# Constant masks by VectorE comparisons in place of GpSimd's affine_select, in a gated attention mix

## The chip, the cores and the metric

The kernel runs on one core of one Trainium2 chip. A core has five engines, each with an instruction stream of its own: TensorE (PE; its weight loads are listed as PEld), VectorE (DVE), ScalarE (ACT), GpSimd (POOL) and SyncE (SP, which here only issues DMAs). They wait for one another by semaphores. The metric is the device time of one execution in microseconds (us), the median of several runs. Beside it stands one execution taken by the hardware profiler, whose records the views of the profile are made of.

## The reference, cut to what matters

The input x has 2048 rows of 512 numbers. Two blocks are computed of it and mixed by a gate for each row.

```
g = sigmoid((x * gate_w).sum(-1))          # one number for each row
a = softmax_attention(x, A_wqkv, A_wo)     # 32 heads of 16, softmax over 2048 keys
b = linear_attention(x, B_wqkv, B_wo)      # phi(t) = (t > 0 ? t + 1 : exp(t)) + 1e-6
out = g * a + (1 - g) * b
```

In block A, for each head, `p = softmax(q k^T / 4)` and `o = p v`; the heads' outputs, side by side, are multiplied by `A_wo`. In block B `kv = phi(k)^T v` and `z = sum(phi(k))` are formed for each head, and `o = phi(q) kv / (phi(q) z)`.

## The kernel before, in words

Block A is most of the work: 32 heads x 2048 queries x 2048 keys of exponentials. Heads are taken in four groups of eight (`t8`), queries in four chunks of 512 (`qc`), keys in 16 blocks of 128. A round handles four of the eight heads of a group (half 0: heads 0, 2, 4, 6; half 1: the others) for one chunk of queries. TensorE makes scores, keys on the partitions and queries along the row, with the four heads in four strips of 32 rows of the array; a strip holds the 16 rows of the wanted head and 16 rows of zeros (tile `Qpad`, four slots). The scores are then turned into exponentials, most of them by ScalarE (L2069, three or two banks of 512 at once, into `PT`), the others by VectorE, which writes an integer whose bits approximate the exponential (L1563, into `DP`), with shifted copies of it made by GpSimd's INT64_ADD (L1607) or by VectorE (L1604). TensorE multiplies `PT` and `DP` with the values (`Vaug`, which carries a column of ones for the sums). Block B's steps, the output projection and the normalisation are woven in between.

The order of instructions on each engine is fixed when the program is built: a planner in the kernel keeps a clock for each engine, adds up estimated durations (`dur`) and picks the next step by them. On the chip each engine works through its list in order. `op(engine, fn, reads, writes, dur)` records one instruction; the waits come from what it reads and writes (L168, L100). TensorE is taken to be in order with itself and waits for no result of its own; VectorE, ScalarE and GpSimd do wait on their own semaphore for an earlier result that they need. One rule more counts here (L530): each GpSimd instruction also waits for the last VectorE instruction recorded before it that reads no PSUM, since the two share a path to SBUF.

The start of the program, which the change touches, runs so:

- ScalarE's queue issues the load of the first 512 rows of x (tile `xn0`, which lies in `PT`), then of half the columns of the other rows (`xnat`, in `phi`). SP's queue issues the three slices of A's weights for the first head group (`wA0`, in `outt`: Q, K, V), six DMA transposes of x into `xT`, then all of A's weights (`wA`) and the gate's weights, later the Q rows for the other `Qpad` slots (L634), and B's weights.
- GpSimd sets `dummy`, `warm` and `identb` (L702, L733, L734), builds the constant masks (L735 to L744), and sets the upper part of `Vaug`, `ones1`, `dev` and `O_sb` (L758 to L762).
- The masks are four tiles. `identb` (128x128) is the identity that TensorE needs to transpose. `maskK` (128x8) has a one where partition p belongs to head column j, that is where 16 j <= p < 16 j + 16. `maskQ` (128x1) is one on the partitions of the even heads. `blockmask` (128x128) is `maskK` with each column repeated 16 times.
- VectorE sets the lower part of `Vaug` (L750 to L752) and three slots of `Qpad` (L754), and sums four columns of `maskK` into `maskQ` (L756).
- TensorE multiplies `warm` nine times (L1877), transposes the first 512 rows of x with `identb` (16 transposes, L692), and VectorE and ScalarE copy them to `xT`, two each (L1907, L1905). Then come the projections of Q and of the first 256 keys, two more multiplications of `warm`, and the first scores. Q goes to `Qpad` slot 0 through `maskQ` (L885) and unmasked to `Qs` (L889); K goes to `KT` (L854, L857), V to `Vaug` (L912, with scaled copies L923).
- The first exponential (L2069) follows the first three scores.

`maskK` and `blockmask` themselves are used much later, in block B (L1025, L1044), and so is `KVbd`, the tile that the change uses as scratch.

Of the kernel before, what the change touches and what calls it, by code (L numbers as in the profile page):

```python
# [9 lines left out]
ALU = mybir.AluOpType  # L10
AX = mybir.AxisListType
# [203 lines left out]
def bass_gated_mix__mha_block__linear_attn_block__prompt_kernel(  # L215
# [16 lines left out]
    NQC = S // 512  # L232
# [16 lines left out]
    with ExitStack() as es:  # L249
# [18 lines left out]
        identb = SB([128, 128], BF16, "identb")  # L268
        maskK = SB([128, 8], FP32, "maskK")
        maskQ = SB([128, 1], FP32, "maskQ")  # L270
        blockmask = SB([128, 128], BF16, "blockmask")
# [11 lines left out]
        Z0 = V20 + 2 * (NG4 - 1) * (V2C + PAD)  # L283
        Vraw = SB([128, Z0 + 32], BF16, "Vaug")
# [30 lines left out]
        KVbd = SB([128, NCC, 128], BF16, "KVbd")  # L315
# [38 lines left out]
        DV = _Eng("dve", SEM("s_dve"))  # L354
        PO = _Eng("pool", SEM("s_pool"))
# [25 lines left out]
        r_gw, r_ident, r_const, r_mask, r_bmask, r_dummy = R("gw"), R("ident"), R("const"), R("mask"), R("bmask"), R("dm")  # L381
        r_maskQ = R("maskQ")
# [3 lines left out]
        r_V = [[R(f"V{p}_{v}") for v in range(NQC)] for p in range(2)]  # L386
# [17 lines left out]
        r_KVbd, r_Zsel = R("KVbd"), R("Zsel")  # L404
# [143 lines left out]
        def op(E, fn, reads=(), writes=(), dur=0.2, issue=None):  # L548
            settle(reads, writes)
            return _emit(E, fn, reads, writes, dur, issue)  # L550
# [140 lines left out]
        def f_tr(o, i):  # L691
# [12 lines left out]
           dur=1.6)  # L704
# [9 lines left out]
        for t in range(1, NQC):  # L714
            for cc in range(NCD):
                dma(xT[:, cc, 512 * t:512 * (t + 1)], x2[512 * t:512 * (t + 1), 128 * cc:128 * (cc + 1)], semXT[cc][t],
                    writes=[r_xT[cc][t]], total_after=16, transpose=True, E=SP, lands=5.5)
# [7 lines left out]
            return [r_xT[c][t] for c in range(NCC)]  # L725


        def select(view, base, pattern, mult, w):

            op(PO, lambda: nc.gpsimd.affine_select(out=view, in_=view, compare_op=ALU.is_ge, fill=0.0, base=base,  # L730
                                                   pattern=pattern, channel_multiplier=mult), reads=[w], writes=[w])

        op(PO, lambda: nc.gpsimd.memset(warm[:], 0.0), writes=[r_warm])  # L733
        op(PO, lambda: nc.gpsimd.memset(identb[:], 0.0), writes=[r_ident])  # L734
        op(PO, lambda: nc.gpsimd.affine_select(out=identb[:], in_=identb[:], compare_op=ALU.not_equal,  # L735
                                               fill=1.0, base=0, pattern=[[-1, 128]], channel_multiplier=1),
           reads=[r_ident], writes=[r_ident])
        op(PO, lambda: nc.gpsimd.memset(maskK[:], 1.0), writes=[r_mask])
        select(maskK[:], 0, [[-16, 8]], 1, r_mask)
        select(maskK[:], 15, [[16, 8]], -1, r_mask)  # L740
        op(PO, lambda: nc.gpsimd.memset(blockmask[:], 1.0), writes=[r_bmask])
        bm = blockmask[:].rearrange("p (j c) -> p j c", c=16)
        select(bm, 0, [[-16, 8], [0, 16]], 1, r_bmask)
        select(bm, 15, [[16, 8], [0, 16]], -1, r_bmask)  # L744
        n0 = NQC * VG

        def ones(g0, g1):
            return Vraw[:, g0 * VG:g1 * VG].rearrange("p (g x) -> p g x", x=VG)[:, :, 0:VG - PAD].rearrange(
                "p g (n c) -> p g n c", c=VC)[:, :, :, 16:17]
        op(DV, lambda: nc.vector.memset(Vraw[:, 0:n0], 0.0), writes=r_V[0], dur=1.2)  # L750
        op(DV, lambda: nc.vector.memset(ones(0, NQC), 1.0), writes=r_V[0], dur=0.2)
        op(DV, lambda: nc.vector.memset(Vraw[:, Z0:Z0 + 32], 0.0), writes=r_V[0], dur=0.1)  # L752
        for i in range(1, NQS):
            op(DV, lambda i=i: nc.vector.memset(Qpad[:, i, :], 0.0), writes=[r_Q[i]], dur=0.49)  # L754

        op(DV, lambda: nc.vector.reduce_sum(maskQ[:, 0:1], maskK[:].rearrange("p (a two) -> p two a", two=2)[:, 0, :], axis=AX.X),  # L756
           reads=[r_mask], writes=[r_maskQ], dur=0.2)
        op(PO, lambda: nc.gpsimd.memset(Vraw[:, n0:Z0], 0.0), writes=r_V[1] + r_V2, dur=4.0)  # L758
        op(PO, lambda: nc.gpsimd.memset(ones(NQC, NG), 1.0), writes=r_V[1], dur=0.4)
        op(PO, lambda: nc.gpsimd.memset(ones1[:], 1.0), writes=[r_ones1], dur=0.1)  # L760
# [880 lines left out]
        for t8 in range(1, NT8):  # L1641
            base = GPR * r_of(t8 - 1, 0)
# [287 lines left out]
        for st, w in ((step_Q(0, 0, early=True), r_wA0[0]), (step_K(0, 0, early=True, on_act=True, n=256), r_wA0[1])):  # L1930
            b = rot_bank()
            pair.append((st, w, b, st.pieces(b)))
        for c in range(2):
            for st, w, b, pcs in pair:
                fns, _, dur, mac, mode = pcs[c]
# [50 lines left out]
        while True:  # L1986
# [20 lines left out]
            while len(us) < SLOTS[g % 2][1]:  # L2007
                if len(us) == 2 and (away or lend is not None):
                    break
                if len(us) == 2 and g > last_stage:  # L2010
                    own, j3 = b0 + 2 in more, peek()
                    load = dve_load(PE.t)
                    if more and load < (RING_LATE if behind_by() > BEHIND else RING_LOAD):
                        js = [j for j in range(4) if j not in [u % 4 for _, u in us]]
                        three = own and len(more) > 1 and load >= TWO_LOAD and j3 in js
                        c = can_claim(PE.t, [j for j in js if not three or j != j3])
# [42 lines left out]
            for c, eb in extras:  # L2059
# [4 lines left out]
                     dur=QK_T, mac=0.053 * len(fns), mode="rows")  # L2064
            for c, eb in extras:
# [5 lines left out]
               reads=[r_bank[b0 + k] for k in range(len(us))], writes=mine + ([r_xn0] if 3 <= g < 5 else []),  # L2071
               dur=d_act(n), issue=0.055 + n * 8.34e-4)
# [59 lines left out]
        while pv_pending:  # L2132
            if not pv_step(PE.t, force=True):
# [9 lines left out]
                 writes=[r_bank[tbank]], dur=0.3)  # L2143
# [3 lines left out]
           reads=[r_bank[tbank], r_OT[NT8 - 1][lastq]], writes=[r_OT[NT8 - 1][lastq]], dur=0.68)  # L2147
# [4 lines left out]
           writes=[r_bad], dur=0.25)  # L2152
# [5 lines left out]
        for k in order:  # L2158
            tb = 4 * lastq + k
            pe_macro([f_mm(bank_ap(free[k]), OT[:, NT8 - 1, 128 * tb:128 * (tb + 1)], woA[:, NT8 - 1, :], start=(k < NPRE))],  # L2160
                     reads=[r_OT[NT8 - 1][lastq], r_woA], writes=[r_bank[free[k]]], dur=MM512)
        for k in range(NPRE, 4):
# [3 lines left out]
               reads=[r_bank[free[k]], r_g], writes=[r_outl[k]], dur=0.6)  # L2166
            dma(out2[128 * tb:128 * (tb + 1), :], outl[:, k, :], semL[k], reads=[r_outl[k]], total_after=16, E=AC)
        for k in range(NPRE):
# [4 lines left out]
               reads=[r_bank[free[k]], r_pre[k], r_g], writes=[r_outl[k]], dur=d_psum(512))  # L2173
            dma(out2[128 * tb:128 * (tb + 1), :], outl[:, k, :], semL[k], reads=[r_outl[k]], total_after=16, E=SP)
            if k == 0:
                op(DV, lambda: nc.vector.scalar_tensor_tensor(out=bad, in0=dev[:, 1, :], scalar=OK_MID - OK_HALF, in1=bad,  # L2176
                                                              op0=ALU.is_lt, op1=ALU.max),
                   reads=[r_dev, r_bad], writes=[r_bad], dur=0.28)
                pe_macro([f_mm(bank_ap(tbank)[0:1, 0:128], ones1[:], bad)], reads=[r_bad, r_ones1],
                         writes=[r_bank[tbank]], dur=0.1)  # L2180
        op(DV, lambda: nc.vector.reduce_max(flag[0:1, 0:1], bank_ap(tbank)[0:1, 0:128], axis=AX.X),  # L2181
           reads=[r_bank[tbank]], writes=[r_flag], dur=0.28)
# [178 lines left out]
```

## Time and profile before

| | before |
|---|---|
| time, median of 3 runs | 678.46 us (678.44 to 678.69) |
| time of the profiled execution | 678.79 us |
| its span, first to last instruction | 677.0 us |
| ScalarE busy | 655.0 us (97%) |
| TensorE busy | 649.5 us (96%) |
| VectorE busy | 565.1 us (83%) |
| GpSimd busy | 343.0 us (51%) |
| mean granted TensorE clock | 0.99 |

The span is shorter than the execution's own time; what lies around it (1.79 us) is start and end of the program. Busy time is that of recorded instructions; a matmul's end is modelled, so a busy TensorE is not TensorE at its peak. In a timeline row stand the start and the length in us, engine, line, operation, output tile <- input tiles, shape and count; in square brackets the idle time ahead of it and what ended that. In a row of the chain stand start, length, and what the chain ran through; "issue" is time in which the engine waited for nothing that the profile shows. In a group's row the part behind the bar is busy time in us and mean ns of one, and then idle time ahead of the group's instructions. L1907 is line 1907 of the kernel; L685 and L692 are the helpers that issue every matmul and every transpose. SPq and ACTq are DMA issues on the queues of SP and ScalarE.

### The profile page before, as it was taken

The page shows a single profiled execution, that of the slowest core. Times are in us where ns is not written, and L with a number is a line of the kernel's source. Part 1 is how long each engine was busy: PE and PEld are TensorE (multiplying, and loading weights), DVE is VectorE, ACT ScalarE, POOL GpSimd, SP SyncE. Part 2 cuts the span into 40 slices and gives each one's busy share as a digit, 9 for nine tenths or more (in the row PEclk, how much of TensorE's full clock was granted, in tenths as well). Part 3 has the DMA queues.
Part 4 walks back from the last instruction along what each step waited for, and adds up shares of the span by engine and source line. Part 5 has one row for each costly group of instructions (what it writes and reads, how often), then busy time and mean ns, then how long its engine had stood idle before and what let it go on. Part 6 is the DMA issues. An engine that isn't in the chain of part 4 may idle for free.

```text
span 677.0 us, 19101 instructions
## 1 busy us (share of the span) xinstructions
PE 649.5 (96%) x8028; PEld 199.0 (29%) x8028; DVE 565.1 (83%) x952; ACT 655.0 (97%) x710; POOL 343.0 (51%) x339
## 2 busy tenths in 40 slices
PE   4999999999999999999999999999999999999997
PEld 2422222333223323333222323233222322222223
DVE  2478889889998987977889999899989987888793
ACT  1999999999999999999999999999999999999996
POOL 2235465453545464544555555555555455656551
PEclk7999999999999999999999999999999999999999
DMA  9800100101000011200001011011102201020111
GB/s 218 229 26 3 32 4 11 25 3 26 10 18 19 9 27 33 53 16 17 19 1 34 18 26 27 10 34 25 35 9 38 53 22 45 12 46 19 28 27 48
DMA packets 44816, 22.96 MB, mean 34 GB/s; under 512 B 33976, under 2 KB 40568, under 8 KB 44728
## 3 DMA queue, kind: packets, MB, share of 16 engines
q1 hardware_dynamic: 42712, 20.12, 13.1%
q10 hardware_dynamic: 2016, 1.57, 0.9%
q8 instruction: 66, 1.08, 0.7%
q14 instruction: 22, 0.18, 0.1%
HBM read 8.00 MB, written 2.10 MB: 15 GB/s over the span
## 4 chain that ended last, share of the span: by engine, by line
ACT 93%; PE 4%; issue 2%; DVE 1%; POOL 0%; POOLq 0%; ACTq 0%
ACT PT L2069 90%; PE ps L685 4%; ACT epool L968 2%; PE ps L692 0%; DVE DP L2171 0%; DVE epool L1402 0%; DVE epool L1403 0%; DVE KT L857 0%; POOL identb L735 0%; DVE DP L2176 0%; DVE flag L2181 0%; POOL identb L734 0%; POOL warm L733 0%; POOL dummy L702 0%; ACT eg L952 0%
## 5 line engine op out<-in xcount | busy, mean ns | idle before, releaser
L2069 ACT ACTIVATE PT<-ps 128x1024 bf16<-128x1024 f32 (+1 forms) x670 | 643.1, 1160 | 1.0 <-PE ps L685 0.9
L1563 DVE TENSOR_SCALAR DP<-ps 128x512 int16<-128x512 f32 x664 | 439.4, 686 | 72.4 <-PE ps L685 66.3
L1607 POOL INT64_ADD DP<-DP x320 | 334.6, 1055 | 307.3 <-DVE DP L1563 223.7
L685 PE MATMUL ps<-Qpad,KT 32*128 32x512 bf16 x2048 | 262.9, 384 | 12.1 <-ACT PT L2069 6.4
L685 PE MATMUL ps<-DP,Vaug 128*32 128x512 f16 x1987 | 203.7, 384 | 1.7 <-DVE oraw L1304 1.5
L685 PE MATMUL ps<-PT,Vaug 128*32 128x512 bf16 x1373 | 169.9, 384 | 0.5 <-DVE Vaug L912 0.5
L685 PEld LDWEIGHTS ps<-Qpad,KT 32*128 32x128 bf16 x2048 | 66.0, 91 | 272.9 <-ACT PT L2069 245.5
L685 PEld LDWEIGHTS ps<-DP,Vaug 128*32 128x32 bf16 x1987 | 49.2, 95 | 61.2 <-issue 37.8
L685 PEld LDWEIGHTS ps<-PT,Vaug 128*32 128x32 bf16 x1373 | 40.6, 95 | 46.9 <-issue 36.0
L685 PE MATMUL ps<-warm 128*32 128x512 bf16 (+2 forms) x221 | 39.9, 391 | 1.1 <-POOL warm L733 1.1
L685 PE MATMUL ps<-xT,wA 128*32 128x512 bf16 x432 | 32.5, 384 | 0.0
L968 ACT ACTIVATE epool<-ps 128x512 bf16<-128x512 f32 x32 | 23.3, 730 | 0.0
L1304 DVE COPY oraw<-ps 128x512 f32<-128x512 f32 x31 | 21.2, 682 | 0.5 <-PE ps L685 0.4
L685 PE MATMUL ps<-wB,xT 128*32 128x512 bf16 x256 | 19.7, 384 | 0.0
L685 PE MATMUL ps<-xT,wB 128*32 128x512 bf16 x256 | 19.7, 384 | 0.0
L685 PE MATMUL ps<-woA,OT 128*32 128x512 bf16 (+1 forms) x226 | 19.1, 384 | 0.0
L973 DVE SCALAR_TENSOR_TENSOR phi<-ps,epool 128x512 bf16<-128x512 f32 x24 | 16.4, 682 | 0.1
L857 DVE CAST KT<-ps 128x512 bf16<-128x512 f32 (+1 forms) x16 | 10.7, 667 | 5.6 <-PE ps L685 5.6
L685 PE MATMUL ps<-wA,xT 128*128 128x128 bf16 x192 | 14.9, 220 | 0.0
L685 PEld LDWEIGHTS ps<-warm 128*32 128x32 bf16 (+1 forms) x221 | 9.9, 98 | 13.7 <-issue 12.1
L912 DVE CAST Vaug<-ps 128x512 bf16<-128x512 f32 x16 | 10.9, 684 | 3.6 <-PE ps L685 3.6
L685 PEld LDWEIGHTS ps<-wA,xT 128*128 128x128 bf16 x192 | 10.8, 98 | 5.4 <-issue 5.0
(104 smaller groups left out, 238.7 us busy)
## 6 DMA issues: line engine op xcount, KB each, us to landing
rbc<-oraw SPq DMA_DIRECT2D x16, 256.0 KB
OT<-in_A_x_dram SPq DMA_DIRECT2D x4, 512.0 KB, 6.5
Qpad<-Qs SPq DMA_DIRECT2D x124, 16.0 KB, 1.8
oraw<-oraw SPq DMA_DIRECT2D x60, 32.0 KB, 1.9
wA<-in_A_wqkv_dram SPq DMA_DIRECT2D x1, 1536.0 KB, 7.0
wB<-in_B_wqkv_dram SPq DMA_DIRECT2D x1, 1536.0 KB, 7.0
out_dram<-outt SPq DMA_DIRECT2D x12, 128.0 KB, 2.0
phi<-in_A_x_dram ACTq DMA_DIRECT2D x3, 256.0 KB, 6.3
```

The lines of the kernel that those rows point to most:

```text
L685: return lambda: nc.tensor.matmul(o, lhsT=l, rhs=r, start=start, stop=stop, skip_group_check=sg)
L857: push(1, [(lambda: nc.vector.tensor_copy(KT[:, par, c0:c1], src), [r_bank[b]], [r_KT[par][t]], d_psum(n), None)])
L912: ops = [(lambda: nc.vector.tensor_copy(v_group(NQC * par + v)[:, :, :, 0:16], src), [r_bank[b]], [r_V[par][v]], d_psum(512), lambda: v_do ...
L968: op(AC, lambda: nc.scalar.activation(epool[:, s, :], bank_ap(b), ACT.Exp), reads=[r_bank[b]], writes=[r_e[s]], dur=0.6, issue=0.48)
L973: (lambda: nc.vector.scalar_tensor_tensor(out=dst, in0=bank_ap(b), scalar=0.0, in1=epool[:, s, :], op0=ALU.max, op1=ALU.add), [r_bank[b], ...
L1304: push(0, [(lambda: nc.vector.tensor_copy(oraw[:, half, :], acc), [r_acc], [r_oraw[half]], d_psum(512), evicted)])
L1563: push(0 if in_group else 1, [(lambda: nc.vector.tensor_scalar(DP[:, i, 512 * k:512 * (k + 1)].bitcast(I16), bank_ap(b), FRAC - Y_BIAS4, Y ...
L1607: ops = (*ops[:4], None, POOL_ADD, lambda z=z, i2=i2, i=i, n=n: nc.gpsimd.int64_add(DP[:, i2, 0:n].bitcast(I64), DP[:, i, 0:n].bitcast(I64 ...
L2069: op(AC, lambda p0=p0, b0=b0, n=n: nc.scalar.activation(PT[:, 512 * p0:512 * p0 + n], ps[:, 512 * b0:512 * b0 + n], ACT.Exp, scale=LN2 / F ...
```

## The change

`identb`, `maskK`, `maskQ` and `blockmask` get the same contents in another way. VectorE writes the numbers 0 to 31 along the columns of a piece of `KVbd` (`cols`: two memsets, then four additions that double the part that is filled), and a transpose in blocks of 32x32 makes of it `rows`, whose value is the partition's number modulo 32. Comparisons of the two give the four diagonal blocks of `identb`; `rows` below 16 gives `maskQ`, and eight comparisons on 32 partitions each give the columns of `maskK`, which GpSimd has set to zero. `blockmask` becomes a GpSimd copy of `maskK` with each column read 16 times. The three memsets for the lower part of `Vaug` go from VectorE to GpSimd. The five affine_selects, the memsets of `maskK` and `blockmask` to one, and the sum into `maskQ` are gone. In the built programs a reconfiguration of GpSimd stood directly ahead of the first affine_select and another ahead of the first INT64_ADD; the changed program has only the second. The lists of TensorE, ScalarE and SP are the same instructions in the same order, and so are those of VectorE and GpSimd behind the setup.

```diff
--- before.py
+++ after.py
@@ -725,36 +725,42 @@
             return [r_xT[c][t] for c in range(NCC)]
 
 
-        def select(view, base, pattern, mult, w):
-
-            op(PO, lambda: nc.gpsimd.affine_select(out=view, in_=view, compare_op=ALU.is_ge, fill=0.0, base=base,
-                                                   pattern=pattern, channel_multiplier=mult), reads=[w], writes=[w])
-
+        cols, rows = KVbd[:, 0, 0:32], KVbd[:, 0, 32:64]
         op(PO, lambda: nc.gpsimd.memset(warm[:], 0.0), writes=[r_warm])
         op(PO, lambda: nc.gpsimd.memset(identb[:], 0.0), writes=[r_ident])
-        op(PO, lambda: nc.gpsimd.affine_select(out=identb[:], in_=identb[:], compare_op=ALU.not_equal,
-                                               fill=1.0, base=0, pattern=[[-1, 128]], channel_multiplier=1),
-           reads=[r_ident], writes=[r_ident])
-        op(PO, lambda: nc.gpsimd.memset(maskK[:], 1.0), writes=[r_mask])
-        select(maskK[:], 0, [[-16, 8]], 1, r_mask)
-        select(maskK[:], 15, [[16, 8]], -1, r_mask)
-        op(PO, lambda: nc.gpsimd.memset(blockmask[:], 1.0), writes=[r_bmask])
-        bm = blockmask[:].rearrange("p (j c) -> p j c", c=16)
-        select(bm, 0, [[-16, 8], [0, 16]], 1, r_bmask)
-        select(bm, 15, [[16, 8], [0, 16]], -1, r_bmask)
+        for j in (0, 1):
+            op(DV, lambda j=j: nc.vector.memset(cols[:, j:j + 1], float(j)), writes=[r_KVbd], dur=0.07)
+        for j in (2, 4, 8, 16):
+            op(DV, lambda j=j: nc.vector.tensor_single_scalar(cols[:, j:2 * j], cols[:, 0:j], float(j), ALU.add),
+               reads=[r_KVbd], writes=[r_KVbd], dur=0.1)
+        op(DV, lambda: nc.vector.transpose(rows, cols), reads=[r_KVbd], writes=[r_KVbd], dur=0.12)
+        for b in range(4):
+            w = slice(32 * b, 32 * b + 32)
+            op(DV, lambda w=w: nc.vector.tensor_tensor(identb[w, w], cols[w, :], rows[w, :], ALU.is_equal),
+               reads=[r_KVbd, r_ident], writes=[r_ident], dur=0.1)
+        op(DV, lambda: nc.vector.tensor_single_scalar(maskQ[:, 0:1], rows[:, 0:1], 16.0, ALU.is_lt), reads=[r_KVbd],
+           writes=[r_maskQ], dur=0.1)
+        op(PO, lambda: nc.gpsimd.memset(maskK[:], 0.0), writes=[r_mask])
+        for b in range(4):
+            w = slice(32 * b, 32 * b + 32)
+            op(DV, lambda w=w, b=b: nc.vector.tensor_single_scalar(maskK[w, 2 * b:2 * b + 1], rows[w, 0:1], 16.0, ALU.is_lt),
+               reads=[r_KVbd, r_mask], writes=[r_mask], dur=0.1)
+            op(DV, lambda w=w, b=b: nc.vector.tensor_single_scalar(maskK[w, 2 * b + 1:2 * b + 2], rows[w, 0:1], 16.0, ALU.is_ge),
+               reads=[r_KVbd, r_mask], writes=[r_mask], dur=0.1)
         n0 = NQC * VG
 
         def ones(g0, g1):
             return Vraw[:, g0 * VG:g1 * VG].rearrange("p (g x) -> p g x", x=VG)[:, :, 0:VG - PAD].rearrange(
                 "p g (n c) -> p g n c", c=VC)[:, :, :, 16:17]
-        op(DV, lambda: nc.vector.memset(Vraw[:, 0:n0], 0.0), writes=r_V[0], dur=1.2)
-        op(DV, lambda: nc.vector.memset(ones(0, NQC), 1.0), writes=r_V[0], dur=0.2)
-        op(DV, lambda: nc.vector.memset(Vraw[:, Z0:Z0 + 32], 0.0), writes=r_V[0], dur=0.1)
+        op(PO, lambda: nc.gpsimd.memset(Vraw[:, 0:n0], 0.0), writes=r_V[0], dur=2.0)
+        op(PO, lambda: nc.gpsimd.memset(ones(0, NQC), 1.0), writes=r_V[0], dur=0.3)
+        op(PO, lambda: nc.gpsimd.memset(Vraw[:, Z0:Z0 + 32], 0.0), writes=r_V[0], dur=0.1)
         for i in range(1, NQS):
             op(DV, lambda i=i: nc.vector.memset(Qpad[:, i, :], 0.0), writes=[r_Q[i]], dur=0.49)
 
-        op(DV, lambda: nc.vector.reduce_sum(maskQ[:, 0:1], maskK[:].rearrange("p (a two) -> p two a", two=2)[:, 0, :], axis=AX.X),
-           reads=[r_mask], writes=[r_maskQ], dur=0.2)
+        op(PO, lambda: nc.gpsimd.tensor_copy(blockmask[:].rearrange("p (j c) -> p j c", c=16),
+                                             maskK[:].unsqueeze(2).to_broadcast([128, 8, 16])),
+           reads=[r_mask], writes=[r_bmask], dur=0.3)
         op(PO, lambda: nc.gpsimd.memset(Vraw[:, n0:Z0], 0.0), writes=r_V[1] + r_V2, dur=4.0)
         op(PO, lambda: nc.gpsimd.memset(ones(NQC, NG), 1.0), writes=r_V[1], dur=0.4)
         op(PO, lambda: nc.gpsimd.memset(ones1[:], 1.0), writes=[r_ones1], dur=0.1)
```

## The prediction

> **What bounds the kernel now.** I read the page first: span, and the costliest group of instructions.
>
> ```profile
> span 677.0 us, 19101 instructions
> ...
> L2069 ACT ACTIVATE PT<-ps 128x1024 bf16<-128x1024 f32 (+1 forms) x670 | 643.1, 1160 | 1.0 <-PE ps L685 0.9
> ```
>
> ScalarE's exponentials fill 643.1 of 677.0 us, and ahead of all 670 of them it was idle 1.0 us in all, 0.9 of that before the first. So once the first exponential starts, ScalarE never waits again, and the end is the start of that first one plus a fixed string of work. Whatever the change does to the time it does by moving the first exponential, or by tearing a hole into the string afterwards. So I looked at the chain that ended last, in its first 15 us, and then at each engine's timeline there.
>
> ```profile
> 1.42 10.86 issue
> 12.28 0.28 POOL identb L735
> 12.56 0.07 POOL maskK L738
> 12.63 0.07 issue
> 12.71 1.86 PE ps L692 x16
> ```
>
> The start of the chain is not ScalarE but GpSimd: from 1.42 to 12.28 us it stands for 10.86 us with nothing shown that it waits for, in front of the first affine_select (L735, the identity matrix). Only then can TensorE transpose x (L692). In the order of the built programs a reconfiguration of GpSimd stands directly ahead of that affine_select, and a second one ahead of the first INT64_ADD; memsets have none. I read the 10.86 us as fetching the code for that operation.
>
> ```profile
> 1.10 1.04 DVE L750 MEMSET Vaug<- 128x1184 uint32 x1 [1.10 <-PEq L2346]
> 2.66 0.17 DVE L751 MEMSET Vaug<- 128x128 bf16 x1 [0.51 <-DVE Vaug L750]
> 2.90 0.07 DVE L752 MEMSET Vaug<- 128x16 uint32 x1
> 2.97 0.82 DVE L754 MEMSET Qpad<- 128x256 uint32 x3
> 13.18 0.16 DVE L756 TENSOR_REDUCE maskQ<-maskK 128x1 f32<-128x4 f32 x1 [9.39 <-POOL maskK L730]
> 13.33 0.69 DVE L1907 COPY xT<-ps 128x512 bf16<-128x512 bf16 x1
> 14.18 0.69 DVE L1907 COPY xT<-ps 128x512 bf16<-128x512 bf16 x1 [0.16 <-PE ps L692]
> 16.88 0.75 DVE L885 TENSOR_SCALAR Qpad<-ps,maskQ 128x512 bf16<-128x512 f32 x1 [2.01 <-PE ps L685]
> ```
>
> VectorE does its setup by 3.79 us and then waits 9.39 us.
>
> ```profile
> 1.08 3.77 PE L685 MATMUL ps<-warm 128*128 128x512 bf16 x9 [1.08 <-POOL warm L733]
> 12.71 1.86 PE L692 MATMUL ps<-identb,PT 128*128 128x128 bf16 x16 [7.85 <-POOL maskK L738]
> 14.50 2.75 PE L685 MATMUL ps<-xT,outt 128*32 128x512 bf16 x32
> 17.18 1.03 PE L685 MATMUL ps<-warm 128*128 128x512 bf16 x2
> 18.15 0.39 PE L685 MATMUL ps<-Qpad,KT 32*128 32x512 bf16 x3
> ```
>
> ```profile
> 18.59 22.06 ACT L2069 ACTIVATE PT<-ps 128x1536 bf16<-128x1536 f32 x18 [0.91 <-PE ps L685]
> ```
>
> The rows name "maskK L738" as releaser; the transposes read identb, so it is L735 that counts. Transposes from 12.71, projections of Q and K from 14.50, scores at 18.15, first exponential at 18.59.
>
> **What is late next, if identb is early: the data.** The x block for the transposes is issued at 0.79 on ScalarE's queue, the three weight slices behind one another on SP's:
>
> ```profile
> 0.79 0.43 ACTq L608 DMA_DIRECT2D PT<-in_A_x_dram  x1
> ```
>
> ```profile
> DMA to landing us min/median/max: 4.0/4.0/4.0
> ```
>
> ```profile
> 0.79 1.66 SPq L608 DMA_DIRECT2D outt<-in_A_wqkv_dram  x3
> ```
>
> ```profile
> DMA to landing us min/median/max: 4.4/5.4/7.0
> ```
>
> These are the loads of PT and of outt. x lands at 0.79 + 4.0 = 4.8; the weights at about 5.2 (Q), 6.7 (K: issued near 1.3, plus 5.4) and 8.9 (V). TensorE's nine warm-up matmuls end at 4.85. So the transposes can start near 4.9, not 12.71: at most 7.8 us of the 10.86 are to be had there. The rest of the load's time is hidden by x.
>
> **The change, part by part.** (1) Five affine_selects and the reconfiguration ahead of them go: the 10.86 us leave the chain. (2) The large memset and two small ones of Vaug leave VectorE (1.04 + 0.17 + 0.07). (3) VectorE gets 20 tiny instructions, nearly all waiting for the one before: two memsets, four additions, a 32x32 transpose, four comparisons into identb, one into maskQ, eight into maskK; then the Qpad memsets as before, and only behind them the first copy of xT (L1907). Everything here is in order, so the copy queues behind all of it. Of the small instructions some stand in VectorE's timeline above, and one in the groups by line:
>
> ```profile
> L956 DVE TENSOR_SCALAR gom<-eg 128x16 f32<-128x16 f32 x1 | 0.1, 110 | 0.0
> ```
>
> A scalar addition or comparison: between 0.11 (L956) and 0.16 (L756, a reduction, above), so 0.14. Memset 0.07 (L752). The transpose and the comparisons of 32x32 have no row; nothing here takes under 0.07, and the 128x512 copy takes 0.69; the nearest in size is L751 with 0.17, so 0.18. The wait from one instruction to its dependent one has two rows in the timeline: 0.07 (L751 to L752: 2.83 to 2.90) and 0.51 (L750 to L751). I take 0.07, since L750 is a large write at the program's start; 0.51 stays as upper bound, none as lower.
>
> Identity: 2 x 0.07 + 4 x 0.14 + 0.18 + 4 x 0.18 = 1.60, and ten waits 0.70: from 1.10 to 3.40. That is 1.4 us ahead of x, so its cost is nothing, by cover of that DMA. maskQ: 0.21 more, 3.61. maskK: GpSimd's memset waits for maskQ and hands back, 0.3 for both (a small memset is about 0.1); then 8 x 0.14 + 7 x 0.07 = 1.61: 5.5. Qpad memsets 0.82: 6.35. The first copy could otherwise go 0.62 behind the first transpose (12.71 to 13.33), at 5.5. So the tiny instructions cost 0.85 us there.
>
> (4) From there on. VectorE's two copies, 2 x 0.69, end at 7.75 (ScalarE's two lie beside them). The second half of the 32 projection matmuls waits for the last copy; all 32 took 2.75. The granted clock:
>
> ```profile
> 4.47:7.88 3.41, 0.38 (x2) 0.00 (x0) 0.00 (x0) 0.00 (x0) 0.00 (x0) 1.00 1.23 276
> 7.88:11.30 3.42, 0.00 (x0) 0.00 (x0) 0.00 (x0) 0.00 (x0) 0.00 (x0) 0.50 1.29 211
> 11.30:14.71 3.41, 2.00 (x20) 1.76 (x24) 1.37 (x3) 0.69 (x2) 2.15 (x8) 0.50 0.64 134
> 14.71:18.12 3.41, 3.41 (x34) 1.07 (x26) 1.40 (x3) 0.85 (x2) 3.41 (x1) 0.50 1.00 368
> ```
>
> (Columns: stretch, length, busy time of PE, PEld, DVE, ACT, POOL, then the granted TensorE clock.) The stall of 7.85 us let the clock fall to 0.50 at 7.88, and the whole start ran at half. With work in every stretch I take 1.00: the half of the matmuls is then 2.75 / 4 = 0.7, its Q part 0.45. L885 starts at 7.75 + 0.15 + 0.45 + 0.25 (drain) = 8.6 and ends, 0.75 later, at 9.35; K and two warm matmuls (0.5) are through by 9.1. Scores at 9.45, the exponential 0.44 behind (18.15 to 18.59): **9.9 instead of 18.59, a gain of 8.7 us.**
>
> (5) Does the rest follow? K of the next 512 keys:
>
> ```profile
> 20.95 0.83 PE L685 MATMUL ps<-xT,outt 128*32 128x512 bf16 x12 [0.29 <-DVE xT L1907]
> ```
>
> ```profile
> 2.49 9.16 SPq L604 DMA_TRANSPOSE xT<-in_A_x_dram  x6
> ```
>
> ```profile
> DMA to landing us min/median/max: 2.9/4.7/7.6
> ```
>
> It would run at 12.2; the first of its two DMA transposes lands at 2.49 + 7.6 = 10.1, the sixth at about 10.4 + 2.9 = 13.3, and it needs the first two of six: 10.1 and some 10.7. It holds, with 1.5 us to spare. These DMAs don't move, so this is the next limit behind mine.
>
> (6) GpSimd itself.
>
> ```profile
> 14.05 5.00 POOL L758 MEMSET Vaug<- 128x5888 bf16 x1
> 19.11 0.65 POOL L759 MEMSET Vaug<- 128x128 bf16 x1
> 19.35 0.41 POOL L760 MEMSET ones<- 128x1 bf16 x1
> 19.39 0.58 POOL L761 MEMSET dev<- 128x256 f32 x1
> 19.91 0.53 POOL L762 MEMSET Osb<- 128x512 bf16 x1
> 41.95 2.06 POOL L1607 INT64_ADD DP<-DP  x2 [21.51 <-DVE DP L1563]
> ```
>
> At 0.85 ns an element the Vaug part taken over (2368) is 2.0 us, from 5.6 to 7.6, far ahead of the first write of V. Then come a strided memset (0.65 in L759), a copy for blockmask (no row; not under nothing, and not over the 0.65 of the slowest memset with its 128 elements; I take 0.3), the 5.00 us memset and the small ones (19.11 to 20.44, 1.3): setup ends near 15, and the code for INT64_ADD is fetched then. It must be there at 41.95 - 8.7 = 33.2; 10.86 from 15 is 26. Cost nothing.
>
> Sum: 677.0 - 8.7 = 668.3 span. The profiled execution took 678.79, so 1.79 lie around the span: 670.1; it lies 0.33 over the median of the runs, 678.46, so 669.8 on the scale of that median.
>
> **Rivals.** *The clock falls all the same.* The stretch 11.30 to 14.71 had 2.00 us of TensorE, mostly transposes, and did not lift the clock; my stretch to 7.88 has 0.4 of warm-up, 0.9 of transposes and only some 0.7 of projections. At half clock from 7.88 the matmuls and warm-ups behind the copy take twice as long: scores near 10.1, and K's second half delays the second exponential by some 0.4; gain 7.6, 670.9. The Trainium skill (TensorE: Matmul & The Clock Gate, Part 4) says that transposes do not count as busy for the clock; the two stretches above fit that. Chance 0.25.
>
> *GpSimd is late for its first add.* The only bound of the second fetch is from the end of setup (20.44) to 41.95, 21.5 us; if it takes all that, or the copy for blockmask needs a fetch too, the adds start at 36.5, 3.3 late: gain 5.4 if nothing buffers it, 673.1. Against it: 10.86 for the first. The Trainium skill (GPSIMD Engine Reference, 2.1 Instruction dispatch) gives about 6 us for a freshly loaded kernel; the trace has 10.86, and I use that. Chance 0.10.
>
> *VectorE's chain is the new bound, to the point of slower.* If a dependent step costs 0.78 (0.51 of wait and 0.27 busy, as long as one Qpad memset) where I have about 0.21, twenty steps end 11.4 later, the first copy is at 17.8, and with the 5.26 us from there to the exponential that the trace has at half clock (13.33 to 18.59) that one starts at 23.0: 4.4 late, 682.9. It decides from about 0.56 a step, where the first copy is back at 13.33. For it is only the row of L751; against it L752. Slower 0.05; a part of it, a gain of 2 to 7, 0.06.
>
> *It doesn't do what it says*: another wait of ten microseconds stands behind the first, and nothing moves. Against it are the DMA landings. Chance 0.03.
>
> **How the numbers follow.** Forecast 0.51: 669.8, its own range 668.8 (no cost of the chain, gain 9.7) to 670.4 (one wait of 0.51 more). Faster by over 0.2% (1.36 us, about what a measurement here can tell from no change): 0.51 + 0.25 + 0.10 + 0.06 = 0.92; within 0.03; slower 0.05. The range, 668.8 to 672.8, holds the forecast and the half clock and leaves out the late add at its full price, the chain and no change, together under 0.2.
>
> **What would show it.** No gap on GpSimd ahead of 5 us; transposes near 4.9; VectorE's last setup instruction near 6.3, with the waits in its chain 0.07; the first exponential near 9.9; granted clock 1.00 after 7.9; INT64_ADD near 33; and ScalarE's idle time ahead of the exponentials still 1 us. It is wrong if the first copy waits for VectorE past 7, if ScalarE shows new idle time in the first 40 us, or if the copies find x late.

## The result and the profile after

| | before | changed |
|---|---|---|
| time, median | 678.45 us (4 runs, 678.21 to 678.69) | 669.4 us (4 runs, 669.29 to 669.63) |
| ratio | | 0.9867, 95% interval 0.985 to 0.9884 |
| time of the profiled execution | 678.79 us | 669.31 us |
| its span | 677.0 us | 667.5 us |
| first exponential (L2069, now L2075) | 18.59 us | 9.10 us |

The kernel is 9.05 us faster by the medians, and 9.5 by the two spans. The difference lies in the profiled executions: that of before is 0.34 over its median, that of the changed kernel 0.09 under its own. From the diff on, line numbers are 6 higher than before.

On the page of the changed kernel, the span and ScalarE's exponentials:

```profile
span 667.5 us, 19111 instructions
...
L2075 ACT ACTIVATE PT<-ps 128x1024 bf16<-128x1024 f32 (+1 forms) x670 | 643.1, 1161 | 0.9 <-PE ps L685 0.7
```

The string of exponentials is the same 643.1 us with 0.9 us of idle time ahead of its members. So the whole change is in where it starts. VectorE's timeline (start, length, line, operation, tiles, count):

```profile
0.80 0.19 DVE L732 MEMSET KVbd<- 128x1 bf16 x2 [0.80 <-PEq L2352]
1.02 0.78 DVE L734 TENSOR_SCALAR KVbd<-KVbd 128x2 bf16<-128x2 bf16 x4
1.83 0.21 DVE L736 STREAM_TRANSPOSE KVbd<-KVbd 128x32 bf16<-128x32 bf16 x1
2.08 0.77 DVE L739 TENSOR_TENSOR identb<-KVbd 32x32 bf16<-32x32 bf16 x4
2.88 0.15 DVE L741 TENSOR_SCALAR maskQ<-KVbd 128x1 f32<-128x1 bf16 x1
3.23 0.14 DVE L746 TENSOR_SCALAR maskK<-KVbd 32x1 f32<-32x1 bf16 x1 [0.20 <-POOL maskK L743]
...
4.75 0.82 DVE L759 MEMSET Qpad<- 128x256 uint32 x3
5.48 1.22 DVE L1913 COPY xT<-ps 128x512 bf16<-128x512 bf16 x2
```

Identity done at 2.85; the tiny instructions follow one another in 0.02 to 0.03 us (1.80 to 1.83, 2.85 to 2.88). The first copy starts as soon as the Qpad memsets let it. TensorE, then ScalarE:

```profile
4.92 1.07 PE L692 MATMUL ps<-identb,PT 128*128 128x128 bf16 x16
6.26 1.67 PE L685 MATMUL ps<-xT,outt 128*32 128x512 bf16 x32 [0.27 <-DVE xT L1913]
7.86 0.61 PE L685 MATMUL ps<-warm 128*128 128x512 bf16 x2
8.66 0.40 PE L685 MATMUL ps<-Qpad,KT 32*128 32x512 bf16 x3 [0.20 <-DVE Qpad L891]
```

```profile
9.10 22.06 ACT L2075 ACTIVATE PT<-ps 128x1536 bf16<-128x1536 f32 x18 [0.74 <-PE ps L685]
```

The 16 transposes started at 12.71 and took 1.86 us; now they start at 4.92 and take 1.07. What they wait for now is x, which landed at 4.88; the last warm-up matmul ends beside it. The row of their weight loads says so:

```profile
4.92 0.90 PEld L692 LDWEIGHTS ps<-identb,PT 128*128 128x128 bf16 x16 [0.79 <-DMA PT<-in_A_x_dram]
```

Of the 9.49 us by which the first exponential moved, 7.79 are the earlier start of the transposes; the other 1.70 are the way from there to the exponential, 4.18 us now instead of 5.88 at the half clock. The granted clock, in the stretches between its decisions (length, busy PE, PEld, DVE, ACT, POOL, then the clock, DMA share and GB/s):

```profile
4.63:8.04 3.41, 3.11 (x50) 1.71 (x50) 2.23 (x6) 1.13 (x3) 3.24 (x5) 1.00 1.28 271
8.04:11.46 3.42, 2.75 (x35) 1.13 (x34) 2.25 (x5) 2.65 (x3) 3.42 (x1) 1.00 1.11 193
```

It stays at 1.00, where before it was 0.50 from 7.88 to 18.12. And GpSimd:

```profile
4.69 2.07 POOL L755 MEMSET Vaug<- 128x2368 bf16 x1 [1.49 <-DVE maskK L748]
...
7.60 0.29 POOL L761 CAST blockmask<-maskK 128x128 bf16<-128x128 f32 x1
...
32.45 2.05 POOL L1613 INT64_ADD DP<-DP  x2 [18.21 <-DVE DP L1569]
```

No stall at the head, and the first add is there when VectorE has its data.

### The profile page after: what moved, and what is told of

Read it like the earlier page. It is cut to its first block, busy times and chain, and to the rows that moved or that the text cites. A ratio compares the mean times of both kernels' runs of the same rounds, so it can differ in the third digit from the quotient of the medians.

```text
span 667.5 us, 19111 instructions
## 1 busy us (share of the span) xinstructions
PE 647.2 (97%) x8026; PEld 198.3 (30%) x8028; DVE 566.5 (85%) x968; ACT 655.0 (98%) x710; POOL 344.6 (52%) x337
## 4 chain that ended last, share of the span: by engine, by line
ACT 94%; PE 4%; DVE 1%; issue 0%; POOL 0%; ACTq 0%
ACT PT L2075 92%; PE ps L685 4%; ACT epool L974 2%; DVE DP L2177 0%; DVE Qpad L759 0%; DVE Qpad L891 0%; DVE KVbd L734 0%; DVE epool L1409 0%; DVE epool L1408 0%; DVE identb L739 0%; DVE maskK L746 0%; DVE maskK L748 0%; DVE xT L1913 0%; DVE KT L863 0%; PE ps L692 0%
## 5 line engine op out<-in xcount | busy, mean ns | idle before, releaser
L2075 ACT ACTIVATE PT<-ps 128x1024 bf16<-128x1024 f32 (+1 forms) x670 | 643.1, 1161 | 0.9 <-PE ps L685 0.7
```

The costliest lines, as they stand in the source:

```text
L2075: op(AC, lambda p0=p0, b0=b0, n=n: nc.scalar.activation(PT[:, 512 * p0:512 * p0 + n], ps[:, 512 * b0:512 * b0 + n], ACT.Exp, scale=LN2 / F ...
```

## The experiments

Two questions stood behind them: is the fetch ahead of identb all that counts, and how near to costing time are the things that the prediction took to be hidden or harmless (VectorE's chain, the clock, the later adds)? In the short diffs `#` stands ahead of a remark, and lines are shortened. The theory is that of the prediction. Each kernel's medians lie beside runs of the kernel before on the same chip. "First copy" is VectorE's first copy to xT, "first exp" ScalarE's first exponential, both in the profiled execution. Each view has the line numbers of its own kernel.

| kernel | median us | ratio to before (95% interval) | first copy | first exp |
|---|---|---|---|---|
| 1 identity by select | 678.54 | 0.9999 (0.9989 to 1.0009) | 13.15 | 17.89 |
| 2 identity and maskQ only | 669.63 | 0.9866 (0.985 to 0.9883) | 5.89 | 9.23 |
| 3 Vaug memsets only | 678.77 | 0.9999 (0.9989 to 1.0008) | 13.02 | 17.90 |
| 4 masks only | 672.51 | 0.9901 (0.9885 to 0.9918) | 7.54 | 12.19 |
| 5 twelve steps | 672.04 | 0.9899 (0.9882 to 0.9915) | 7.78 | 12.47 |
| 6 25 steps | 676.02 | 0.9959 (0.9945 to 0.9973) | 10.26 | 15.24 |
| 7 one more fetch | 669.57 | 0.9865 (0.9848 to 0.9881) | 5.56 | 9.54 |
| 8 short chain | 670.89 | 0.9882 (0.9865 to 0.9898) | 5.50 | 9.14 |
| 9 late add | 676.2 | 0.9965 (0.9953 to 0.9978) | 5.48 | 9.09 |
| 10 late masks | 669.31 | 0.9867 (0.985 to 0.9883) | 4.94 | 8.65 |
| 11 twelve steps, warm | 671.41 | 0.9895 (0.9879 to 0.9912) | 7.78 | 11.11 |
| 12 add first | 669.35 | 0.9863 (0.9846 to 0.9879) | 5.58 | 9.35 |

### Which part of the change counts (1 to 4)

**1, identity by select**: the comparisons for identb out, its affine_select back.

```diff
 memset(identb, 0)
+memset(maskK, 0)                      # GpSimd, moved up
+affine_select(identb, not_equal, fill=1.0)
-4 x tensor_tensor(identb block, cols, rows, is_equal)
```

> The changed kernel with one affine_select put back, that of identb; maskK's memset stands ahead of it, so that VectorE's chain is not held up, and everything else stays as changed. My theory, that the code fetch ahead of identb is all that counts: the whole gain is gone, 678.4 us, within 0.6, with the first affine_select near 12.2 us and the first exponential near 18.5. Rival, that the four other selects or the moved memsets carry part of the gain: between 670 and 677 us.

678.54 us: nothing of the gain is left. On GpSimd:

```profile
12.11 0.28 POOL L732 TENSOR_SCALAR_AFFINE_SELECT identb<-identb 128x128 bf16<-128x128 bf16 x1 [10.97 <-issue]
```

One affine_select costs what five did; the stall ahead of the first is the price, not the operations.

**2, identity and maskQ only**: the kernel before, with these two tiles made by VectorE.

```diff
-affine_select(identb, ...)
-reduce_sum(maskQ, four columns of maskK)
+cols, rows, identb blocks, maskQ      # VectorE, as in the change
```

> The kernel before with identb and maskQ alone made by VectorE; maskK and blockmask still come from affine_select with the fetch ahead of them, and Vaug's memsets stay on VectorE, behind identb and maskQ. My theory: the gain is there, 669.4 us within 0.6, since nobody waits for maskK early; GpSimd then ends its setup near 20.3 and fetches again, and the adds are wanted at 32.4, which holds if the second fetch takes no more than the first, 10.9. Rival, that the other masks count: 674 us or more. Rival, that the second fetch takes longer than 12.1: the adds come late by the excess.

669.63 us. The stall is still there, in front of maskK:

```profile
11.93 0.44 POOL L730 TENSOR_SCALAR_AFFINE_SELECT maskK<-maskK 128x8 f32<-128x8 f32 x2 [10.73 <-issue]
```

It lasts as long as ever and costs nothing, since nobody waits for maskK that early. 1 and 2 together settle the theory: what counted was that identb stood behind the stall.

**3, Vaug memsets only**: the kernel before, with this move alone.

```diff
-VectorE: memset(Vaug[0:n0], 0); memset(ones, 1); memset(Vaug[Z0:], 0)
+GpSimd:  the same, behind the masks
```

> The kernel before with nothing changed but the three memsets of Vaug, which go to GpSimd behind the masks. My theory: no change, 678.4 us within 0.5, as VectorE waits for identb anyway. Rival, that the move itself gains: 677.2 us, by the 1.3 us that leave VectorE.

678.77 us: no change, as expected.

**4, masks only**: the changed kernel with these memsets back on VectorE.

```diff
+VectorE: memset(Vaug[0:n0], 0); memset(ones, 1); memset(Vaug[Z0:], 0)
-GpSimd:  the same
```

> The changed kernel with the three memsets of Vaug back on VectorE, behind the comparisons and ahead of the Qpad memsets. My theory: VectorE's chain is just what the first copy waits for, so 1.3 to 1.8 us more in it (1.04 + 0.17 + 0.07, and the 0.51 of wait behind the large one) move the first copy from 5.5 to 6.8 to 7.3, and the time to 670.6 to 671.1 us. Rival, that the chain has slack there: 669.4 us.

672.51 us, 3.1 over the changed kernel and 1.4 over my upper figure. VectorE's timeline:

```profile
4.93 1.04 DVE L755 MEMSET Vaug<- 128x1184 uint32 x1 [0.31 <-issue]
6.49 0.17 DVE L756 MEMSET Vaug<- 128x128 bf16 x1 [0.51 <-DVE Vaug L755]
6.73 0.07 DVE L757 MEMSET Vaug<- 128x16 uint32 x1
6.80 0.82 DVE L759 MEMSET Qpad<- 128x256 uint32 x3
7.54 1.22 DVE L1913 COPY xT<-ps 128x512 bf16<-128x512 bf16 x2
```

The copy is 2.06 us later, a little more than expected; the first exponential is 3.09 later. The rest is the clock:

```profile
5.07:8.48 3.41, 1.20 (x24) 0.92 (x26) 2.83 (x8) 1.07 (x2) 0.79 (x2) 1.00 1.29 241
8.48:11.90 3.42, 3.42 (x37) 1.14 (x29) 1.62 (x3) 0.37 (x1) 3.42 (x1) 0.50 1.07 203
```

TensorE had 1.20 us of work in a stretch of 3.41, and the next stretch ran at 0.50. So the move is worth nothing alone (3) and 3.1 us beside the new masks (4): once the fetch is gone, VectorE's chain is what the first copy waits for.

### The chain and the clock (5, 6, 8, 10, 11)

**5, twelve steps** and **6, 25 steps**: dependent additions of zero more in VectorE's chain.

```diff
+for _ in range(12):                   # 25 in kernel 6
+    tensor_single_scalar(cols[:, 0:1], cols[:, 0:1], 0.0, add)
 transpose(rows, cols)
```

> The changed kernel with twelve dependent additions of zero more in VectorE's chain, ahead of the transpose, about 0.2 us each: identb at about 5.3 instead of 2.9, the first copy at 7.9 instead of 5.5. My theory, that the chain is at the edge: 2.2 to 2.4 us more, 671.7 us. If the clock falls at the end of the stretch in which TensorE then idles, up to 1 us more, 672.7. Rival, that the chain has slack behind the x load: 669.4 to 670 us.

> The same with 25 additions: identb at about 7.8, the first copy at 10.4. Without the clock 4.9 us more, 674.3 us; with the clock at 0.50 for some microseconds, as before the change, 675.3 us or a little more. If the steps cost more than 0.2 us each, as the slower rival had it (0.78 each), 689 us.

The first copy comes 2.30 and 4.78 us later, 0.19 a step: the chain has no slack, and a step costs 0.19, not 0.78. The first exponential comes 3.37 and 6.14 later, and the times are 672.04, between the figures without and with the clock, and 676.02, above the one with it. In both the granted clock went to 0.50 (in kernel 5 from 8.47 for one stretch, in kernel 6 from 8.24 for two). Whether those 1.1 and 1.4 us are the clock's was tried next.

**11, twelve steps, warm**: kernel 5 with work for TensorE in the gap.

```diff
 16 transposes of x
+6 x matmul(warm)                      # into a bank that is free
```

> The twelve extra steps again, with six warm-up matmuls more on TensorE behind the 16 transposes, in time in which it waits for VectorE's copy (5.3 to 8.5 us). With the steps alone the first copy came 2.3 us later than in the changed kernel, but the first exponential 3.4 us later, and the granted clock was 0.50 from 8.5 to 11.9. My theory: the 1.1 us beyond the steps are the clock's, and these matmuls keep it at 1.00: first exponential near 11.4, 671.6 us or a little less, 0.8 to 1.1 us under the steps alone profiled beside 672.76. Rival, that the 1.1 us have another cause: no change in the exponential's start, 12.4.

The copy starts at 7.78 as in 5, the first exponential at 11.11 instead of 12.47. First of two lines: kernel 5; second: kernel 11.

```profile
8.46 2.75 PE L685 MATMUL ps<-xT,outt 128*32 128x512 bf16 x32 [2.11 <-DVE xT L1918]
```

```profile
8.46 1.48 PE L685 MATMUL ps<-xT,outt 128*32 128x512 bf16 x32 [0.82 <-DVE xT L1918]
```

The same 32 projections, from the same start, in 2.75 us at the low clock and 1.48 at the full one. So the rival about the clock is a real mechanism, shown by taking it away; the changed kernel, whose TensorE works 3.11 us of the stretch, keeps the clock. The medians of 5 and 11 alone (672.04 and 671.41) would not show it, since the intervals of their ratios overlap; the rows do. The runs of 5 spread from 671.31 to 672.76, those of 11 from 671.29 to 671.61; I read this as stretches that fall elsewhere from one execution to the next, so that 5 loses by them in some only.

**8, short chain**: the Qpad memsets on GpSimd, maskK's comparisons behind the first copies.

```diff
-VectorE: 8 comparisons for maskK; 3 x memset(Qpad)      # ahead of the first copy
+GpSimd:  memset(maskK, 0)                               # moved up, behind identb's
+GpSimd:  3 x memset(Qpad)
+VectorE: 8 comparisons for maskK                        # behind Q's two copies
+GpSimd:  copy to blockmask                              # behind these
```

> The changed kernel with a shorter chain on VectorE: the Qpad memsets go to GpSimd, and the eight comparisons for maskK behind the first copies. The first copy then waits for TensorE alone. My theory: the first copy comes at 5.35 instead of 5.48, and since the projections also wait for ScalarE's copies, 0 to 0.2 us are gained, 669.2 to 669.4 us, hardly to be measured. Rival, that the chain still bounds the start: 668.6 us or less.

A miss: 670.89 us, every run (670.11 to 671.71) slower than all of the changed kernel. The start is as expected, first exponential at 9.14; but VectorE's next piece is late, and ScalarE's second exponential with it. VectorE, then ScalarE:

```profile
10.31 0.15 DVE L1941 TENSOR_SCALAR maskK<-KVbd 32x1 f32<-32x1 bf16 x1
10.49 0.42 DVE L854 CAST KT<-ps 128x256 bf16<-128x256 f32 x1
```

```profile
9.14 1.45 ACT L2075 ACTIVATE PT<-ps 128x1536 bf16<-128x1536 f32 x1 [0.74 <-PE ps L685]
11.41 2.79 ACT L2075 ACTIVATE PT<-ps 128x1536 bf16<-128x1536 f32 x2 [0.82 <-PE ps L685]
```

The copy of K's second half (9.66 in the changed kernel) stands behind the last comparison. While TensorE waits for it the stretch gets thin, and the next one ran at 0.50:

```profile
8.92:12.34 3.42, 2.14 (x37) 1.05 (x38) 2.48 (x12) 2.38 (x2) 3.42 (x1) 1.00 0.99 181
```

The runs of kernels 4, 5 and 8 fall in two groups by their mean granted clock: with 0.999 or 1.0 they took 671.27 (4), 671.31 and 671.58 (5), 670.11 and 670.31 us (8), with 0.996 or 0.997 some 0.9 to 1.6 us more. So without the clock kernel 8 loses 0.8 us, the 0.82 of ScalarE's row, and kernel 4 1.9, about the 2.06 of its copy. In kernel 6 the mean does not order the runs.

**10, late masks**: the same comparisons behind the first writes of V.

```diff
-8 comparisons for maskK, copy to blockmask               # behind Q's two copies
+8 comparisons for maskK, copy to blockmask               # behind the first writes of V
```

> The short chain again, with maskK's eight comparisons behind the first writes of V instead of ahead of the copy of K's second half. In the run with the short chain that copy came at 10.49 instead of 9.66, ScalarE then waited 0.82 us for its second exponential, and the clock fell for one stretch. My theory: that placement was the whole loss, so this one is as fast as the changed kernel, 669.2 to 669.6 us, with the first exponential near 9.1. Rival, that the memsets of Qpad on GpSimd cost the time: 670.5 us or more.

669.31 us: the placement was the whole loss. It isn't faster than the changed kernel by more than the runs differ. Its profiled execution starts earlier (8.65), and so do its transposes (4.50 against 4.92):

```profile
4.50 0.90 PEld L692 LDWEIGHTS ps<-identb,PT 128*128 128x128 bf16 x16 [0.38 <-DMA PT<-in_A_x_dram]
```

They wait for x, not for VectorE. In this execution x landed at 4.46, in that of the changed kernel at 4.88, though the edit does not touch its load. So the load of x, with the warm-up beside it, is what bounds the start now.

### The later adds, and whose code is fetched (7, 9, 12)

**7, one more fetch**: an affine_select that changes no value, at the end of GpSimd's setup.

```diff
 memset(O_sb, 0)
+affine_select(blockmask, ...)         # a reconfiguration ahead of it, one behind it
```

> The changed kernel with one affine_select more on blockmask at the end of GpSimd's setup; it changes no value, but needs a code fetch at 14.3 us, and INT64_ADD needs another one behind it. The first start shows how long a fetch takes beside less traffic: my theory 10.9, so the select near 25.3 and the adds near 36.4 instead of 32.4. The time then says what a late first add costs: 673.4 us if nothing buffers it, 669.4 if the plan has slack. Rival, a fetch of some 6 us: both fetches end by 27, and no loss.

669.57 us, no loss. GpSimd's timeline:

```profile
22.49 0.34 POOL L770 TENSOR_SCALAR_AFFINE_SELECT blockmask<-blockmask 128x128 bf16<-128x128 bf16 x1 [8.19 <-issue]
```

Here the stall lasted 8.2 us. The adds began when VectorE was ready, so the reconfiguration between select and adds cost at most 10.1 us (22.84 to 32.90); more this run doesn't say.

**9, late add**: 14 us of memsets of an unused tile, then a small add of zero.

```diff
 memset(O_sb, 0)
+4 x memset(OBT2, 0)
+int64_add(z, z, 0)                    # z: 64 columns of O_sb, read as 16 INT64
```

> The changed kernel with four memsets of an unused tile (128x4096, about 3.5 us each) and one small INT64_ADD of zero at the end of GpSimd's setup; they change no value. The small add's start shows the second fetch by itself, behind setup's end near 28.3: 8 us as in the run with one more fetch (start near 36.4), or 10.9 (39.2). The plan wants the first real add at 32.5, so it comes 4 to 7 us late. My rival of a late add said that the time pays all of it: 673 to 676 us. The other theory, that the plan has other work between: less than half of it, 669.4 to 671.5 us, with idle time of ScalarE near 35 to 42 us if anything is lost.

676.2 us, but not for the reason expected. GpSimd, then VectorE:

```profile
14.18 14.22 POOL L770 MEMSET OBT<- 128x4096 bf16 x4
28.55 0.21 POOL L772 INT64_ADD Osb<-Osb  x1
```

```profile
22.49 2.43 DVE L933 TENSOR_SCALAR Vaug<-Vaug 128x288 bf16<-128x288 bf16 x1
24.84 0.62 DVE L1966 COPY xT<-ps 128x1024 bf16<-128x1024 bf16 x1
25.39 3.10 DVE L933 TENSOR_SCALAR Vaug<-Vaug 128x288 bf16<-128x288 bf16 x1
```

The small add stands 0.15 us behind the memsets, with its reconfiguration between: no fetch to be seen. And the loss came before any add was due: VectorE's scaling of V (L933), 0.23 us in the kernel before (L923 there), took 2.43 and 3.10, each until the GpSimd memset of 3.5 us beside it was over (at 24.84 and 28.40). The Q copy behind them, and TensorE behind that, were 4 us late, and the clock added to it:

```profile
25.10:28.52 3.42, 0.00 (x0) 0.00 (x0) 3.42 (x3) 1.04 (x1) 3.30 (x1) 1.00 1.27 214
28.52:31.93 3.41, 2.75 (x21) 0.70 (x21) 0.77 (x2) 1.45 (x1) 0.21 (x1) 0.50 0.89 273
```

TensorE did nothing in one stretch, and the two after it, to 35.35, ran at 0.50; ScalarE was idle 3.69 us in one piece and then 2.30 in three more. The probe disturbed what it was to measure; the price of a late add is not measured, and the run tells of something else (below).

**12, add first**: the kernel before and one small add.

```diff
 memset(identb, 0)
+int64_add(z, z, 0)                    # z: 64 columns of identb, read as 16 INT64
 affine_select(identb, ...)            # all masks, Vaug and Qpad as before
```

> The kernel before, all masks by affine_select and Vaug's memsets on VectorE, with one small INT64_ADD of zero ahead of the first affine_select; it changes no value. In the built program GpSimd's only reconfiguration then stands ahead of this add, and none ahead of the selects or the later adds. In the run with the late add, a small add stood 0.1 us behind its reconfiguration, while an affine_select stood 8.1 us behind its own with one more fetch, and 10.9 in the kernel before. Theory A, that the code set with INT64_ADD needs no fetch here and serves affine_select too: the add near 1.5 us, identb by 2.1, the first exponential near 8.7 to 9.1, 669.0 to 669.4 us, as fast as the changed kernel without its 20 small instructions. Theory B, that the first reconfiguration of a program costs about 10.9 us whatever it fetches, and the 0.1 us came from its place late in the program: 678.4 us or some tenths more.

669.35 us. GpSimd:

```profile
1.32 0.21 POOL L736 INT64_ADD identb<-identb  x1
1.69 0.29 POOL L737 TENSOR_SCALAR_AFFINE_SELECT identb<-identb 128x128 bf16<-128x128 bf16 x1 [0.16 <-POOL identb L736]
```

```profile
9.35 1.45 ACT L2071 ACTIVATE PT<-ps 128x1536 bf16<-128x1536 f32 x1 [0.74 <-PE ps L685]
```

Theory A's outcome: with the add first, GpSimd is configured for it, and affine_select runs 0.16 us behind it without a stall. The kernel before, with one instruction more, is as fast as the changed one: the intervals of the ratios, 0.9846 to 0.9879 and 0.985 to 0.9884, lie on one another.

## Why the prediction was right, point by point

It forecast 669.8 us, 668.8 to 672.8; 669.4 was measured, by the mechanism forecast. That the two lie so near is in part luck. The first exponential came 0.8 us earlier than forecast, but only 0.4 of that shows in the time: the prediction took off 0.33 for a profiled execution that lies over its median, and that of the changed kernel lies 0.09 under its own. Its steps:

- **The end is the first exponential's start plus a fixed string.** Shown: 643.1 us and 0.9 us idle again, and the last of the exponentials ended 9.5 us earlier, as the first began.
- **The stall of 10.86 us is a code fetch for affine_select, and only identb makes it count.** Kernels 1, 2, 7, 9 and 12 show that the stall goes with a reconfiguration made for affine_select and not with one made for INT64_ADD; 1 and 2 show that it costs time through identb alone. That code is fetched in it stays a reading: no row shows it, and the two DMA queues of kind instruction move nothing from 1.42 to 12.28 us in the kernel before. That INT64_ADD has a fetch of the same size was wrong, see the adds.
- **x is next.** Transposes at 4.92 against 4.9, with x landed at 4.88 against 4.8.
- **VectorE's chain is hidden up to identb and costs 0.85 at the first copy.** Right in kind, too dear: identity at 2.85 instead of 3.40, first copy at 5.48 instead of 6.35. It began 0.3 earlier (0.80), a wait inside it cost 0.02 to 0.05 instead of 0.07, an addition 0.17 instead of 0.14. Where VectorE waits for TensorE (kernel 10), the copy comes 0.44 behind the first transpose; by that it could have come at 5.36 here, so the chain cost some 0.12 (an estimate). Kernel 4 shows how near the edge that is.
- **From the copy to the exponential 3.55.** It was 3.62, by terms that nearly cancel: VectorE's copies took 1.22 instead of 1.38, the wait from them to Q's copy 1.06 instead of 0.85. No run shows the 0.15 and the 0.25 of drain in that sum by themselves. So the first exponential came at 9.10, not 9.9, all by the chain.
- **The clock stays at 1.00.** It did, but with luck: the prediction gave TensorE about 2.0 us (0.4, 0.9 and 0.7) in the stretch that decides, and kernel 8's clock fell after 2.14. The trace has 3.11, since the copy came earlier than forecast. So the rival deserved more than its 0.25 on the prediction's own numbers; kernels 4, 5, 6 and 11 show it at work.
- **GpSimd is late for its first add.** It was not (32.45, when VectorE had the data). The rival's premise, a second fetch of 10.86 or more, was wrong in size: none is seen in kernels 9 and 12. What a late add would cost stays open.
- **VectorE's chain to the point of slower.** The 0.51 was not a start-up effect, as I took it: kernel 4 has it again, 6.49, behind the same large memset, and nowhere in the tiny instructions. 0.19 a step (kernels 5, 6), far from the 0.56 that decide.
- **The forecast's own range.** Its ends don't add up: without the chain's 0.85 the gain is 9.55, not 9.7, which gives 668.9, and 0.51 more gives 670.3. The chances named for what lies outside the wide range come to as much as 0.24, not under 0.2.

What the prediction did not ask is whether the masks had to leave GpSimd at all: kernel 12 has the gain without VectorE's 20 instructions.

## What to carry to other kernels

When a kernel is one unbroken string of work on its bounding engine, look at what starts the string: a change gains there, at most the distance to the next late input, or loses by a hole that it tears into the string (kernels 8 and 9). A wait ahead of GpSimd's first use of an operation may be a code fetch; before rewriting the operation, see who really waits for it, and whether a set of code that the kernel loads anyway serves it. When a stall goes, check that TensorE keeps working in the gap that is left: in kernels 4, 5, 6 and 8 the clock made the loss larger than the gap.

## What the runs showed of the hardware that I had not expected

- Ahead of an affine_select behind its own reconfiguration GpSimd was idle 11.12 us in the kernel before (10.86 of them behind the reconfiguration), 10.97 and 10.73 in kernels 1 and 2, and 8.19 in 7; behind a small INT64_ADD 0.16. The Trainium skill (GPSIMD Engine Reference, 2.1 Instruction dispatch) has a first call to freshly loaded code pay about 6 us with no instruction to show for it; the second half agrees, the size doesn't. Why INT64_ADD pays nothing, whether its code stays loaded between executions or is there from the start, no run here tells apart.
- A GpSimd memset can hold up a VectorE operation from SBUF to SBUF to its own end: 0.23 us became 2.43 and 3.10 in kernel 9, while a copy out of PSUM between them took 0.62. The Trainium skill (SBUF — State Buffer, Who interferes with whom) names it an exclusive lock on a shared pair of ports that is held for the whole instruction; the ends of the two rows agree with that.
- The clock fell after stretches of 3.41 us in which TensorE was busy for 0.38 (kernel before), 0.64 (kernel 6), 1.06 (kernel 5), 1.20 (kernel 4) and 2.14 us (kernel 8), and stayed after 2.40 (kernel 11), 2.75 and 3.11 (changed kernel). Once at 0.50 it was not lifted after 1.71 (kernel 6) and 2.75 us (kernel 9), but was after 3.41 and 3.42. Whether transposes count in full, no run here tells.
- Behind VectorE's memset of 1184 words the next dependent instruction waited 0.51 us (before and kernel 4), behind the tiny ones 0.02 to 0.05.
